# Orders drawn up anew, a narrow product of the state, and two transfers moved to ScalarE's queue, in an adaLN block with linear attention and an MLP

## The chip, the core and the metric

The kernel runs on one core of a Trainium2 chip. A core has five engines that run their own instruction streams: TensorE (PE, matmuls; its weight loads are listed apart as PEld), VectorE (DVE), ScalarE (ACT), GpSimd (POOL) and SyncE (SP), which here only issues transfers. ScalarE can issue transfers too, on a queue of its own. The metric is the device time of one execution in microseconds; the comparisons are of medians of several runs.

## What is computed

One block on S = 2048 tokens of D = 576 features, all in float32. The six modulation vectors come from one matrix product; then linear attention with 32 heads of 18 features, then an MLP with F = 4608.

```python
mod = (_silu(c) @ w_mod).reshape(c.shape[0], 6, 1, -1)
sa, ca, ga, sb, cb, gb = (mod[:, i] for i in range(6))
h = _layernorm(x) * (1 + ca) + sa
# attention: qkv of h @ wqkv; phi(t) = where(t > 0, t + 1, exp(t)) + 1e-6
kv  = einsum("bhsd,bhse->bhde", phi(k), v)     # the state, summed over the tokens
z   = einsum("bhsd->bhd", phi(k))
o   = einsum("bhqd,bhde->bhqe", phi(q), kv) / (einsum("bhqd,bhd->bhq", phi(q), z)[..., None] + 1e-6)
x = x + ga * (o @ wo)
h = _layernorm(x) * (1 + cb) + sb
x = x + gb * (_silu(h @ w1) @ w2)
```

## The kernel before

**Precision.** TensorE takes float32 operands in two ways here. Plain f32 products are two instructions each in the trace. All large products are done instead in fp32r, one instruction each, with every operand split into a rounded part "hi" and the rest "lo" = full - hi; a product is then hi x hi + hi x lo + lo x hi. ScalarE makes the hi part (a copy with rounding, `w_hi`, `split_h`, `k_split`, `split_w`), VectorE or GpSimd the lo part (a subtraction, `w_lo`, `sub_hi` at L121).

**Tiles.** The tokens are 16 tiles of 128, in four blocks of 512; the features are KC = 4 chunks of 128 and a fifth of 64.

**Head (0 to about 36 us).** ScalarE's queue issues two small transfers of c (L269, L270). SP's queue issues x's first two tiles (`load_x`, L260) and then w_mod: `load_mod_cols(k0, k1)` fetches columns of the four full chunks into `mods` (L287) and of w_mod's last 64 rows into `tmod` (L285, one transfer for each of the two pieces). It is called for the first HEAD = 2 column chunks, and again for the other three. Then come w_qkv (`load_w`) and the rest of x. TensorE runs warm-up matmuls on a tile of ones (`warm_up`, L412) while these land. VectorE adds up w_mod times silu(c) chunk by chunk (`mod_sum`, L360 for the first, L362 for the others), TensorE sums over the partitions (`mod_mm`, L371: `mod_tail` for tmod, then `mod_sums`), VectorE writes the columns (`mod_cols`, L381). With them the normalised and transposed x is modulated and split into hT, and the product for k of tiles 0 and 1 begins (`k_part`, L407). `A.activation(warm, ..., Exp)` (L431) makes ScalarE load the table of the exponential early.

**Attention, first pass (to about 216 us).** For each tile t: `k_proj`, `v_proj`, `q_proj` (their matmuls are in `x_passes`, L226) and the transposes of the next block (L214). `kv_mm(t)` (L588) adds this tile's part of the state: for each of five groups j of seven heads (126 columns) two matmuls, with v's hi and lo parts as weights. The moving operand of both is 256 columns wide: 128 of phi(k)'s hi part, then 128 of its lo part. The two halves of the result lie side by side in a bank of PSUM (`kvp`) and are added after the last tile (L720 and the line after it). So there are 16 x 5 x 2 = 160 matmuls.

**Attention, second pass (to about 345 us).** The state and w_o become one matrix per tile of features; GpSimd forms `prod` (L1195), `pn` (L752) and the copy of pn's last columns (L754) for each tile, TensorE transposes pn (L811) and multiplies (L226). Evacuations of the PSUM tiles `big` are L825 and, for the first MLP groups, L901.

**MLP (the rest).** Products by a scheme with sums of blocks of the operands (L1323 up, L1396 down, L1404 the additions into acc), with operands streamed back from DRAM.

**The order of the work.** TensorE runs in program order. For the other engines ORDERS holds an order by hand, up to about 402 us: number n is the engine's n-th instruction in the order in which the program states them, and `arrange` chains them in the order of the list. After that, `manual_schedule(engines=ENGINES)` runs all engines in program order. The numbers that are spoken of below:

- VectorE: 9 and 10 copies of silu(c)'s last part (L435), 14 ve (L183), 16 and 17 normalising x (L193), 18 mod_sum's first step (L360), 19 and 20 the next two; 21 and 31 mod_cols (L381); 24 to 27 mod_sum for the other columns; 29 and 30 w_lo of w_k's chunks 0 and 1 (L315), 43 of chunk 2; 33, 34, 36, 37 statistics of x (L178), 32 lo of hT's chunk 2 (L121); 76 to 79 normalising x of the next block, 123 a sum for the next modulation vectors (L519); 461 lo of the second-phase hT's chunk 3 (L121), 472 a sum of blocks (L1137), 477 and 465 other lo parts, 475, 484 and 483 additions into acc (L901).
- ScalarE: 3 the early exponential (L431), 11 the copy of tmod's last columns (L368), 15 and 17 hi of hT's chunks 2 and 3 (L205), 28 the exponential of the first k (L326), 30 and 31 hi of w_v's chunks 3 and 4.
- GpSimd: 28, 31, 35, 38, 42 prod, 29, 32, 36 pn, 30 and 33 pn's copies for tiles 2 and 3, 11 and 12 lo of w_v's chunks 3 and 4 (L315, L317).

Of the kernel before, what the change touches and what calls it, by code (L numbers as in the profile page):

```python
# [16 lines left out]
P = 128  # L17
# [5 lines left out]
def kernel(ctx: ExitStack, tc, A_x, A_wqkv, A_wo, B_x, B_w1, B_w2, c, w_mod, out):  # L23
# [7 lines left out]
    nc = tc.nc  # L31
# [4 lines left out]
    S, D = x.shape  # L36
# [6 lines left out]
    KC = D // P  # L43
    HG = 7 * DH
# [7 lines left out]
    def f32(ap):  # L52
# [1 line left out]

    ORDERS = {
        "PE": """
            0-105 114 106-108 115 109-113 116-2585
        """,
        "DVE": """
            2-3 1 0 4 6-7 11-12 8 5 13-14 18 15 9 16 10 17 19-24 29 25 28 26-27 30-31 43-44 33-34 36-37 35 38 32 39  # L60
            41 40 45 42 47 46 50 48-49 62-63 51 64 52 65-66 57 87 67 58 53 59 56 84-85 60 80 86 88 55 83 81 68-69 82
            70-72 122 73 54 74 61 89 75-76 123 78-79 91 77 90 92 124 93-94 96-97 125 98 126 100 127 99 95 103 101
            104-105 102 108 106-107 109-111 132-133 135 134 136 138-139 137 141-142 140 143-144 112-113 146-147 145
            114 148 117 115 149 118 116 119-121 128 131 129-130 150-151 224 222-223 225-226 152-154 157 155 158 156
            159 162 176 160-161 177-179 163 180 165 228 164 181 227 166-167 169-170 168 171-173 193-194 196 195 197
            199 198 200 202 201 203-205 174 206 175 207 182 185 209 183 208 186 188 187 210 184 189 192 190 211 191
            212-213 216 214 217 215 218 220 219 221 229-230 232-233 231 234-237 240 238-239 241-243 246 244 247 245
            248-249 252 250-251 253-255 258 256-257 259 262 260-261 263 266 268 267 270 269 271 264-265 272-273
            275-277 281 274 279 282 280 278 283-285 288 286 289 303 295-296 290 306 302 307 291 314 292 315 297 323
            298-299 293 308 300 324 294 304 331 309-310 287 311 301 312 305 332 316 340 313 317-321 341 325 322 351  # L70
            326-329 333 352 362 334-336 330 337 363 343-344 338 370 345-346 339 347 349 342 348 371 380 350 353-361
            381 398 364-369 372 399 416 373-375 377 376 378 417 424 385 382 384 379 387-388 391-392 394 425 402 386
            389 403 390 404-406 393 407 413 383 408 397 395 409-411 396 414 418 415 412 419-422 400-401 423 426-428
            432 429 431 430 435 433-434 437-440 445 441 446 442 444 443 436 447-451 454 452-453 455 469 466 456 467
            463-464 457 468 458 471 459-460 475 477 484 462 483 472 465 461 478 473 485 474 470 486 480 479 495 487
            482 488 492 481 490 476 493 489 491 494 500-501 497 503 529 499 496 498 510-511 502 506 504-505 507-509
            523 515 512-514 518 528 516-517 527 519 521-522 520 524-526 531 530 533 532 534-535
        """,
        "Activation": """
            0-2 4-9 11 10 3 12 16 19 13 15 14 18 21 17 20 26-27 24 22 29 23 28 25 30-33 55 35 37 59 39 58 42 40 38  # L80
            43 36 41 44 56-57 50 53-54 51-52 45 34 60-61 46 48 47 49 62-63 65-67 64 69 68 70 72 71 73-75 77-78 76 79
            81 80 82-84 93 85 95 87 86 96 88 94 89-92 97 99 98 100-102 104-105 103 106 108 107 109 149 110-112 152
            150-151 153 113-114 116-117 115 118 120 119 121-122 131 123-124 133-134 132 126 125 127-130 135 137 136
            138-139 141-142 140 145 143 146 144 147-148 154-155 157-158 156 159 161 160 162-182 184 183 186 185 188
            187 189-191 193-195 192 196-198 200 202 199 201 203-208 217 212 209 214 213 210 216 219 211 215 224 234
            220 218 239 221-222 225 223 245 235 231-232 256 226 228 230 233 227 229 236 240 237-238 270 241 243 246
            248-250 242 244 247 272 251-254 257 255 278 266 260 262-263 267 265 268 259 269 271 264 258 261 293 273
            305 274-276 281 283 282 277 284 279 307 285-287 296 289 280 288 290 292 291 301-302 299 297-298 303 300
            304 306 294-295 308-311 313 312 315-316 314 322-323 317 320 318-319 321 344 341 324 338 325-326 343 342
            327 339 345 328 330 329 340 332 331 347 333-334 336-337 335 348-349 346 353 350 354-356 351-352 358 357  # L90
            359 387 365 364 363 368 360-362 369 371 374 370 372 366 376 367 373 378 375 377 384 389 379 385 381 380
            382-383 386 388 390-395 397 396
        """,
        "Pool": """
            3 6 0 4-5 2 7 9 8 10-15 20 16-17 19 18 21-26 34 28 27 31 29-30 35 32 38 36 42 33 37 45 39-40 48 43-44 51
            46 41 47 55 49-50 58 52-53 61 85 56 73 57 54 59 77 60 62-63 80 64 74 65 68 75 69 78 66 72 70 79 67 76 81
            71 82-84 95 90-93 86-88 94 101 89 103 105 99-100 97 106-107 121 98 96 102 123 104 108-111 124 114 125
            113 112 115 118 116 119-120 117 122 126-128
        """,
        "SP": """  # L100
            0-25 57 30 26 31 29 32 27 39 28 55 33-34 56 53 40 54 41-46 35-38 47-52 61 63 58 64 60 66 62 59 65 67 69
            68 70-71 76 75 74 72-73 77-82 85 83-84 86-88 95 91 89 92 97 93 90 98 94 96 99-100 102 101 105 104 119
            103 118 117 106-107 110 108 112 109 111 113-116 123 120-122
        """,
    }

# [173 lines left out]
    def load_mod_cols(k0, k1):  # L280
        c0, c1 = k0 * P, min(k1 * P, D)
        for k in range(KC):
            if k == 2:
                for a in range(2):
                    nc.sync.dma_start(tmod[a * 64 : a * 64 + 64, 0, c0:c1], w_mod[KC * P : D, a * D + c0 : a * D + c1])  # L285
# [18 lines left out]
    def mod_ps(k):  # L304
        return kvp[k // 2][:, k % 2, :]
# [276 lines left out]
    def kv_mm(t):  # L582

        pkt, vt = pk[t % 2], vx[t % 2]
        for j in range(NHC):
            o = mod_ps(j)
            for h in range(2):
                T.matmul(  # L588
                    o, vt[:, j, h, :], pkt[:, :, j * HG : j * HG + P],
                    start=(t == 0 and h == 0 and j % 2 == 0), stop=(t == NT - 1 and h == 1),  # L590
                    skip_group_check=True,
                )
# [97 lines left out]
    with tc.manual_schedule(engines={mybir.EngineType.PE}):  # L690
# [77 lines left out]
        for j in range(KC + 1):  # L768
            psm = ps2()
            n = wo_rows[j]  # L770
# [780 lines left out]
        ws.update({g: Weights(g) for g in range(2, NG)})  # L1551
        for u in units[:2]:
            do_unit(*u)
    arrange()
    with tc.manual_schedule(engines=ENGINES):
        for u in units[2:]:
            do_unit(*u)
        for work, tokens in TAIL:
            unit.plain_down(work)
            run(tokens.split(), (unit, behind2), ())  # L1560
    psC.release()
    for p in (rs, ph, pf, pu, w2p, wqp, edge, wp, hTa, accp):
        p.release()
# [28 lines left out]
```

## Time and profile before

| | |
|---|---|
| median of 3 runs | 1142.06 us (1140.82 to 1143.03) |
| profiled execution | 1139.88 us, of it 1138.1 us from the first to the last instruction |
| TensorE clock granted | 1.000 |
| TensorE idle before its instructions, first 50 us / 200 to 402 us | 4.4 / 2.9 us |

The profile is of one execution. Section 1 of the page gives busy time per engine, section 4 the chain of work that ended last, followed back from the last instruction. In the timeline and in lists of groups a row has the start and length in microseconds, the engine, the line, the operation, what it writes and reads, and the count. A row of several instructions runs from the first start to the last end. A note in brackets tells how long the engine was idle before and who ended that. Matmuls are pipelined: the printed length of one is longer than the distance to the next.

### The profile page before, as it was taken

To read this page: it belongs to the slowest core of one execution; us is meant where nothing else is said; L and a number is where in the kernel's file an instruction comes from. 1 tells how busy PE (TensorE), PEld (TensorE's weight loads), DVE (VectorE), ACT (ScalarE), POOL (GpSimd) and SP (SyncE) were. 2 spreads that over 40 slices of the span, in tenths; PEclk is the share of its full clock that TensorE was granted. 3 is DMA by queue.
4 is the path that set the end of the run, shared out by engine and by line. 5 is a ranking of instruction groups with operands and counts; after the bars stand their busy time and mean duration, and the time that the engine had idled before them with its cause. 6 is when DMAs were issued, how large, how long until landed. Compare 5 with 4: busy or idle time off the path is not lost.

```text
span 1138.1 us, 19287 instructions
## 1 busy us (share of the span) xinstructions
PE 1126.6 (99%) x7033; PEld 1041.0 (91%) x7033; DVE 970.6 (85%) x1543; ACT 538.8 (47%) x1112; POOL 649.4 (57%) x743
## 2 busy tenths in 40 slices
PE   8999999999999999999999999999999999999998
PEld 8999999999998889999999999999999999999998
DVE  7866743685879889999999999999999999999996
ACT  6643442547556544445444444454454444444441
POOL 2100000373715767766775777677767767776776
PEclk9999999999999999999999999999999999999999
DMA  9521100223359976977968779769678697697684
GB/s 281 198 84 33 42 7 1 71 84 115 141 194 340 350 262 252 359 270 267 346 262 330 300 257 350 273 255 363 265 284 332 265 342 285 256 344 275 258 306 156
DMA packets 58813, 269.03 MB, mean 236 GB/s; under 512 B 5724, under 2 KB 21856, under 8 KB 35680
## 3 DMA queue, kind: packets, MB, share of 16 engines
q1 hardware_dynamic: 58708, 267.80, 63.8%
q8 instruction: 56, 0.92, 0.3%
q14 instruction: 37, 0.30, 0.1%
q10 hardware_dynamic: 12, 0.00, 0.0%
HBM read 250.12 MB, written 16.78 MB: 235 GB/s over the span
## 4 chain that ended last, share of the span: by engine, by line
PE 93%; DVE 2%; DMA 1%; POOL 1%; ACT 1%; issue 0%; DVEq 0%; POOLq 0%
PE up L1323 34%; PE down L1396 32%; PE psK L226 12%; PE big L226 6%; PE big L896 2%; PE small L885 2%; PE kvp L588 2%; PE small L214 1%; DMA hT<-hd 1%; PE big L811 1%; PE psT L214 1%; PE kvp L412 1%; DMA raw<-in_w_mod_dram 1%; PE up L1426 1%; PE down L1426 1%; POOL prod L1195 0%
## 5 line engine op out<-in xcount | busy, mean ns | idle before, releaser
L1404 DVE TENSOR_TENSOR acc<-down,acc 128x576 f32<-128x576 f32 x330 | 246.2, 753 | 14.6 <-PE down L1396 5.3
L1323 PE MATMUL up<-hT,w 128*128 128x512 f32 x916 | 239.4, 390 | 0.1
L1323 PEld LDWEIGHTS up<-hT,w 128*128 128x128 f32 x916 | 164.5, 188 | 25.0 <-DMA hT<-hd 0.3
L1358 POOL TENSOR_TENSOR s<-f,f 128x256 f32<-128x256 f32 x66 | 51.6, 782 | 162.0 <-ACT f L1339 162.0
L1396 PE MATMUL down<-w,hb 128*128 128x288 f32 x792 | 120.6, 294 | 0.0
L1396 PE MATMUL down<-w,hc 128*128 128x288 f32 x792 | 120.6, 294 | 0.0
L1396 PEld LDWEIGHTS down<-w,hb 128*128 128x128 f32 x792 | 113.8, 188 | 5.1
L1396 PEld LDWEIGHTS down<-w,hc 128*128 128x128 f32 x792 | 113.7, 188 | 5.1
L121 DVE TENSOR_TENSOR w<-v,w 128x288 fp32r<-128x288 f32 (+1 forms) x170 | 114.4, 682 | 0.5 <-ACT w L1057 0.5
L1404 DVE TENSOR_TENSOR U<-down,U 128x576 f32<-128x576 f32 x132 | 99.5, 754 | 17.5 <-PE down L1396 15.6
L226 PE MATMUL psK<-w,hT 128*128 128x352 f32 (+3 forms) x506 | 106.2, 336 | 0.5 <-POOL w L317 0.5
L1323 PE MATMUL up<-room,w 128*128 128x512 f32 x348 | 91.0, 390 | 0.0
L1377 POOL TENSOR_TENSOR hc<-s,hc 128x512 fp32r<-128x512 f32 x66 | 89.4, 1354 | 0.0
L226 PEld LDWEIGHTS psK<-w,hT 128*128 128x128 f32 x506 | 82.0, 189 | 6.8 <-POOL w L317 0.7
L1339 ACT ACTIVATE f<-f 128x512 f32<-128x512 f32 x102 | 64.4, 631 | 48.9 <-DVE f L1344 26.5
L184 POOL TENSOR_TENSOR rstd<-ve,neghalf 128x4 f32<-128x4 f32 (+3 forms) x10 | 9.8, 977 | 134.5 <-DVE ve L183 134.4
L1342 DVE TENSOR_TENSOR f<-up,p 128x512 f32<-128x512 f32 x102 | 69.6, 683 | 12.8 <-PE up L1323 11.9
L1065 ACT CAST w<-v 128x288 fp32r<-128x288 f32 x85 | 36.7, 434 | 75.4 <-PE down L1396 65.9
L1362 POOL TENSOR_TENSOR f<-f,s 128x256 f32<-128x256 f32 x66 | 50.7, 769 | 36.3 <-DVE hb L1377 25.9
L1323 PEld LDWEIGHTS up<-room,w 128*128 128x128 f32 x348 | 62.5, 188 | 9.4
L1396 PE MATMUL down<-w,hd 128*128 128x288 f32 x396 | 63.0, 294 | 0.9 <-DVE acc L1404 0.9
L1396 PE MATMUL down<-w,ha 128*128 128x288 f32 x396 | 63.0, 294 | 0.0
(310 smaller groups left out, 2529.4 us busy)
## 6 DMA issues: line engine op xcount, KB each, us to landing
hT<-hd SPq DMA_DIRECT2D x66, 1280.0 KB, 5.9
hT<-hd SPq DMA_DIRECT2D x45, 1024.0 KB, 5.3
room<-hd SPq DMA_DIRECT2D x35, 1280.0 KB, 5.6
room<-hd SPq DMA_DIRECT2D x20, 1024.0 KB, 5.3
v<-in_B_w_dram SPq DMA_DIRECT2D x17, 576.0 KB, 6.7
v<-in_B_w_dram SPq DMA_DIRECT2D x17, 512.0 KB, 7.0
hd<-S SPq DMA_DIRECT2D x6, 1024.0 KB, 4.3
xt<-in_A_x_dram SPq DMA_DIRECT2D x16, 288.0 KB, 3.1
```

Source lines behind the costliest of these rows:

```text
L121: return V.tensor_sub(lo, full, f32(hi))
L214: T.transpose(ps[:, i * P : (i + 1) * P], xt[i][:, cidx * P : (cidx + 1) * P], ident)
L226: T.matmul(ps, xpart(a), wpart(b), start=n == 0, stop=n == len(XW) - 1)
L1065: A.copy(self.w2[n][:, 0], src)
L1323: T.matmul(ps, left, right, start=first and m == 0, stop=m == len(seq) - 1, skip_group_check=True)
L1339: A.activation(self.f[i, k], self.f[i, k], AF.Silu)
L1342: V.tensor_add(f, self.bank[bank[1]], self.p1)
L1358: G.tensor_add(self.s[:, 0:1], half(i, 0, 1), half(i, 1, 1))
L1362: G.tensor_sub(half(i, 1, 0), half(i, 1, 0), self.s[:, 1:2])
L1377: eng.tensor_sub(t[:, :, 1, :], src, f32(t[:, :, 0, :]))
L1396: T.matmul(ps[:, p, :HALF], self.a[i, n][:, u, p * P : (p + 1) * P], self.w.w2[n][:, v], start=n in (1, 5, 7, 6) and j == 0, stop=j == 2, ...
L1404: V.tensor_add(dst, ps[:, :, :HALF], dst)
```

## The change

Three edits, and the lists of orders that go with them.

1. `kv_mm`: the matmul with v's lo part as weights (h = 1) takes only the 128 columns of phi(k)'s hi part; lo x lo is left out. The other stays 256 wide. The number of instructions is the same.
2. `load_mod_cols`: on its first call the two transfers of w_mod's last 64 rows are issued by ScalarE, behind c's two, in place of SP. ScalarE's numbers from 2 on grow by two, SP's from 6 on fall by two.
3. `arrange()` is called at the end, and TensorE's list has one number more.
4. The lists for VectorE, ScalarE, GpSimd and SP are new throughout; in TensorE's, two transposes stand one matmul later.

The first lines of each list and those that are spoken of, in the numbering of each version:

```diff
         "PE": """
-            0-105 114 106-108 115 109-113 116-2585
+            0-106 114 107-109 115 110-113 116-2586
         "DVE": """
-            2-3 1 0 4 6-7 11-12 8 5 13-14 18 15 9 16 10 17 19-24 29 25 28 26-27 30-31 43-44 33-34 36-37 35 38 32 39
-            41 40 45 42 47 46 50 48-49 62-63 51 64 52 65-66 57 87 67 58 53 59 56 84-85 60 80 86 88 55 83 81 68-69 82
-            70-72 122 73 54 74 61 89 75-76 123 78-79 91 77 90 92 124 93-94 96-97 125 98 126 100 127 99 95 103 101
...
-            432 429 431 430 435 433-434 437-440 445 441 446 442 444 443 436 447-451 454 452-453 455 469 466 456 467
-            463-464 457 468 458 471 459-460 475 477 484 462 483 472 465 461 478 473 485 474 470 486 480 479 495 487
+            0 3 2 1 4 6-7 11 8 12-13 9-10 14-16 18 17 5 19-22 30 23-24 28-29 25-27 43 31 44 33-34 36 35 37-38 32 39
+            41 40 42 45-47 50 48-49 62-63 51-53 57 84 64 55 58 65 59 86 66 85 87 60 56 80 67 88 81 83 68 82 69 71 70
+            72 122 73-74 61 89 54 75 78 76 90 77 79 123 91 124 92-93 96-97 125 98 94 126-127 100 99 95 101 103-104
...
+            440 445 441 446 443 442 444 447-451 455 454 453 452 466 456 467 469 457 464 471 458-460 475 472 462 461
+            463 478 473 477 484 483 485-486 479 468 480 474 487 470 465 493 488 495 490 476 489 482 492 481 491 494
         "Activation": """
-            0-2 4-9 11 10 3 12 16 19 13 15 14 18 21 17 20 26-27 24 22 29 23 28 25 30-33 55 35 37 59 39 58 42 40 38
+            0-4 6-8 11 9-10 12 5 13-14 18 21 15-16 20 19 17 23 28 22 29 24-25 31 26 30 27 32-33 37 34-35 38-39 57 59
...
         "Pool": """
-            3 6 0 4-5 2 7 9 8 10-15 20 16-17 19 18 21-26 34 28 27 31 29-30 35 32 38 36 42 33 37 45 39-40 48 43-44 51
+            6-7 0 3 8 2 4-5 9-15 20 16-17 19 18 21-27 34 28 31 29 35 30 32-33 38 36 42 37 39 45 48 40 43-44 51 46-47
...
         "SP": """
-            0-25 57 30 26 31 29 32 27 39 28 55 33-34 56 53 40 54 41-46 35-38 47-52 61 63 58 64 60 66 62 59 65 67 69
+            0-23 55 28-29 24 26 25 27 30 37 31-32 52 51 53-54 38-44 33-36 45-50 59 61 58 64 62 56 60 63 57 65 67 66
...
@@ load_mod_cols
                 for a in range(2):
-                    nc.sync.dma_start(tmod[a * 64 : a * 64 + 64, 0, c0:c1], w_mod[KC * P : D, a * D + c0 : a * D + c1])
+                    queue = nc.sync if k0 else nc.scalar
+                    queue.dma_start(tmod[a * 64 : a * 64 + 64, 0, c0:c1], w_mod[KC * P : D, a * D + c0 : a * D + c1])
@@ kv_mm
         for j in range(NHC):
-            o = mod_ps(j)
+            o = mod_ps(j).rearrange("p (a q) -> p a q", a=2)
             for h in range(2):
+                n = 2 - h
                 T.matmul(
-                    o, vt[:, j, h, :], pkt[:, :, j * HG : j * HG + P],
+                    o[:, :n], vt[:, j, h, :], pkt[:, :n, j * HG : j * HG + P],
@@ the end of the kernel
-    arrange()
     with tc.manual_schedule(engines=ENGINES):
...
             run(tokens.split(), (unit, behind2), ())
+    arrange()
     psC.release()
```

Numbers of ScalarE and SP in the text are those of the version before.

More of the change, by code (lines that the diff above doesn't have):

```diff
@@ L78 @@
+            529 500-501 499 497 496 498 510 503 502 511 507 506 504-505 508 515 509 514 527 513 512 518 528 519
+            516-517 523 520-522 524-526 531 530 533 532 534-535
         """,
         "Activation": """
[L80 to L82 removed]
```

56 lines of the change are left out of this document (28 added, 28 removed).

## The prediction

> **What bounds the kernel now.** I read the page first, then the list of TensorE's waits, then a table of stretches, and only then the timeline around each wait.
>
> ```profile
> span 1138.1 us, 19287 instructions
> ...
> PE 1126.6 (99%) x7033; PEld 1041.0 (91%) x7033; DVE 970.6 (85%) x1543; ACT 538.8 (47%) x1112; POOL 649.4 (57%) x743
> ...
> PE 93%; DVE 2%; DMA 1%; POOL 1%; ACT 1%; issue 0%; DVEq 0%; POOLq 0%
> ```
>
> TensorE is busy 1126.6 of 1138.1 us and has 93% of the chain that ended last. Time can leave this kernel in two ways only: TensorE does less, or it waits less. The waits are few:
>
> ```profile
> PE psK L407 <- DVE hT L121: 1.4, 1, 1.4
> PE big L811 <- POOL pn L754: 1.0, 1, 1.0
> PE down L1396 <- DVE acc L1404: 0.9, 1, 0.9
> PE small L885 <- DVE hT L121: 0.6, 1, 0.6
> PE psT L214 <- DVE xt L193: 0.3, 1, 0.3
> ```
>
> ```profile
> 50.00:100.00 50.00, 50.00 (x329) 47.37 (x329) 34.53 (x66) 19.90 (x39) 1.01 (x1) 1.00 0.20 62
> 345.00:369.00 24.00, 23.20 (x149) 21.11 (x148) 23.00 (x34) 14.63 (x28) 11.25 (x10) 1.00 0.91 332
> ```
>
> The columns are the length, then busy time of PE, PEld, DVE, ACT and POOL. From 50 to 100 us TensorE is never idle; a new order of the other engines has nothing to win there. At 345 to 369 us VectorE is busy 23.00 of 24.00 us, so there its order counts. The largest waits that an order can touch are in the head (L407, 1.4), at the first transposes of the second phase (L811, 1.0) and at L885 (0.6).
>
> **The narrow product.** kv_mm issues 160 matmuls (L588), 80 of which shrink from 256 to 128 columns. Both the product and its weight load are in the rows:
>
> ```profile
> L588 PEld LDWEIGHTS kvp<-pk,vx x160: 187/188/193, 36.4 to 203.2; 128*128 128x128 f32 x160
> L588 PE MATMUL kvp<-pk,vx x160: 277/282/496, 36.4 to 203.3; 128*128 128x256 f32 x160
> L371 PEld LDWEIGHTS kvp<-ones,hT x20: 186/192/192, 9.5 to 18.5; 128*128 128x128 f32 x20
> ```
> ```profile
> 36.36 1.26 PEld L588 LDWEIGHTS kvp<-pk,vx 128*128 128x128 f32 x10
> 9.50 0.97 PEld L371 LDWEIGHTS kvp<-ones,hT 128*128 128x128 f32 x8 [0.17 <-DVE hT L362]
> 9.50 1.10 PE L371 MATMUL kvp<-ones,hT 128*128 128x64 f32 x8
> 11.28 1.42 PEld L412 LDWEIGHTS kvp<-ones 128*128 128x128 f32 x12
> 386.81 1.82 PE up L1323 x8
> ```
>
> What a matmul costs in a stream is its pitch, not its printed 282 ns. Ten loads in 1.26 us, the last of them 0.19 long, give (1.26 - 0.19) / 9 = 119 ns for 256 columns; 512 columns take 1.82 / 8 = 228 ns. So 256 more columns cost 109 ns, and on that line 128 columns would come at 119 - 54 = 65 ns. But the plain f32 products of the head show a floor: 64 columns run at (0.97 - 0.19) / 7 = 111 ns (L371), and 128 columns at (1.42 - 0.19) / 11 = 112 ns (L412), the same for half the columns. Something that each pair of load and matmul has to go through takes 111 ns, and the load of kv_mm lasts as long (188) as theirs (192). I take 111 ns, since the weight tile is the same 128x128 of four bytes, and keep 65 ns as the other end: 80 x (111 - 119) = -0.6 us, against 80 x (65 - 119) = -4.3. The upper end is the pace of an f32 product, which is two such instructions, 2 x 112 = 224 ns: +8.4 us.
>
> A rule speaks for the floor: the Trainium skill, "TensorE: Matmul & The Clock Gate", section "LDWEIGHTS (loading the stationary operand)", lets a load take its columns over 1.2 GHz, 107 ns for 128. By it the sum of this part would be 80 x (107 - 119) = -1.0 us instead of -0.6, and the two f32 rows agree with it to 5 ns.
>
> **The two transfers on ScalarE's queue.** They leave SP's queue (1.18 us of issuing) and go behind c's two on ScalarE's, ahead of the table load and the silu:
>
> ```profile
> 1.40 0.70 ACTq L270 DMA_DIRECT2D crow<-in_c_dram  x1
> 2.13 1.28 ACT L430 ACT_TABLE_LOAD   x1 [2.13 <-issue]
> 3.00 1.18 SPq L285 DMA_DIRECT2D tmod<-in_w_mod_dram  x2
> 5.33 0.18 ACT L430 ACTIVATE sc<-psT 128x5 f32<-128x5 f32 x1 [1.92 <-PE psT L428]
> 7.97 0.53 PEld L371 LDWEIGHTS kvp<-z,tmod 128*128 128x128 f32 x4
> tmod<-in_w_mod_dram SPq DMA_DIRECT2D x2, 64.0 KB, 4.0
> ```
>
> At 0.70 each they push the table load to 3.5-4.8 us, and the silu waits for TensorE until 5.33 anyway: no cost while that 0.5 us of cover lasts, and up to 0.7 if each issue took twice as long. No gain either: tmod, issued at 3.0-4.2 and landing 4.0 later, is there by 7.6, while TensorE is in its warm-up matmuls until 7.97. What follows on SP's queue starts up to 1.2 us sooner, but VectorE, not a landing, sets the pace there, as the next rows show. I take 0.
>
> **The orders in the head.** VectorE's new list puts the copies of sc (9, 10) and ve (14) before mod_sum's first step (18), which stood ahead of GpSimd's power and filled its 1.00 us:
>
> ```profile
> 5.65 1.00 POOL L184 TENSOR_TENSOR rstd<-ve,neghalf 128x2 f32<-128x2 f32 x1 [1.63 <-DVE ve L183]
> 6.12 0.49 DVE L360 TENSOR_SCALAR hT<-hT,sc 128x512 f32<-128x512 f32 x1 [0.56 <-DMA hT<-in_w_mod_dram]
> 12.74 0.43 DVE L121 TENSOR_TENSOR hT<-raw,hT 128x256 fp32r<-128x256 f32 x1 [0.47 <-ACT hT L205]
> 17.09 0.75 DVE L315 TENSOR_TENSOR w<-acc,w 128x576 fp32r<-128x576 f32 x1
> 20.25 1.53 DVE L178 BATCH_NORM_STATS2 st<-xt 128x6 f32<-128x288 f32 x4
> 21.94 0.37 DVE L121 TENSOR_TENSOR hT<-raw,hT 128x256 fp32r<-128x256 f32 x1
> 29.55 1.82 POOL L317 TENSOR_TENSOR w<-acc,w 64x576 fp32r<-64x576 f32 x1
> ```
>
> Now 18 stands behind the power: ve some 0.25 later, and 0.49 of work that is no longer under it, less 0.3 for the two copies that no longer follow it: the first column sums are about 0.45 us late. Next, w_lo 1 (30, the 0.75 at 17.09) moves from a place where VectorE waited for TensorE to one ahead of five steps on the path; it takes over a wait of 0.47 there, so the second sums are 0.45 + 0.75 - 0.47 = 0.7 late. ScalarE then makes both casts (17, 15) after three modulations instead of the first of them (15) before. That is hidden: the four statistics at 20.25 still stand before chunk 2's difference at 21.94, so L407's wait of 1.4 us is not removed but takes some of the delay. What is late next is ScalarE's copy for GpSimd's two differences, and with them TensorE at L226: I take +0.8 us there. At 49.5 us the wait of 0.3 for xt goes, because 78, 76, 77 and 79 now precede 123, which waits for a transfer: -0.3. Head: +0.5 us, with -1 (the 1.4 us wait shrinks after all) and +2 (nothing of the delays is taken up) as its ends.
>
> **The orders later on.** GpSimd:
>
> ```profile
> 229.97 1.17 POOL L752 TENSOR_TENSOR pn<-acc,r 128x576 f32<-128x576 f32 x1
> 235.96 0.40 POOL L754 COPY pn<-pn 128x64 f32<-128x64 f32 x2
> ```
>
> The copy that ends pn of tile 3 (33) is ready at 231.14 but stands behind 38, 36 and 42 until 235.96, and TensorE waits for it. The new list has 33 ahead of these three. The wait goes: -1.0 us. Copy 30 now goes behind 35, one product of 1.4 us, and has about that much to spare.
>
> VectorE, at L885's wait:
>
> ```profile
> 352.81 0.62 ACT L1092 CAST hT<-S 128x512 fp32r<-128x512 f32 x1
> 353.61 0.76 DVE L901 TENSOR_TENSOR acc<-big,acc 128x576 f32<-128x576 f32 x1
> 355.92 1.76 DVE L1137 TENSOR_TENSOR S<-S 128x512 f32<-128x512 f32 x1
> 357.94 0.68 DVE L121 TENSOR_TENSOR hT<-S,hT 128x512 fp32r<-128x512 f32 x1
> 362.21 6.55 PE L896 MATMUL big<-w,hs 128*128 128x288 f32 x48
> ```
>
> Chunk 3's difference (461, at 357.94) could start at 353.4, when its cast ends. The new list moves it ahead of 477, 484, 483 and 465; it then ends near 356, before TensorE asks: -0.6 us. The price is that the two evacuations 484 and 483 (L901) go back by some 4 us, to about 360, with L896 needing their banks at 362.2. Between -0.7 and 0 (the wait moves on).
>
> All other moves trade places within work that TensorE does not wait for; the bound on them is the wait at L1396 that could go too (-0.9), and new waits, which no row can show (rival 4). The movement of the call of arrange and the one matmul more in TensorE's list change no order: 0.
>
> **Sum:** -0.6 + 0 + 0.5 - 1.0 - 0.6 = -1.7 us; the profiled execution's 1138.1 us of span becomes 1136.4. Around its span that execution has 1.8 us (1139.88), and the median of the three runs is 1142.06, 2.2 above it; I subtract from the median: **1140.4 us**, 0.15% less.
>
> **Rivals.**
>
> 1. The narrow product streams with no floor, at 65 ns: -4.3 instead of -0.6, -5.4 in all, 1136.7 us. For it speaks the straight line from 512 to 256 columns, against it the 64 columns at 111 ns, though those are f32, not fp32r. The Trainium skill, on the same page, section "Back-to-back issue gap", states 81 ns for pairs of load and matmul at 128 columns; by that figure this part would be -3.0 us.
>
> 2. The orders take more: L1396's 0.9 and 1.0 of L407's wait go too. -1.7 - 1.9 = -3.6, 1138.5 us. For it: both are waits for VectorE; against it: the statistics still stand ahead of chunk 2, and L1396 lies behind the end of the list.
>
> 3. Slower: below 256 columns an fp32r product falls back to the pace of an f32 one, 224 ns. Place: all 80 matmuls; +8.4 instead of -0.6, 1149.4 us. No fp32r product under 256 columns is in this trace, so no row excludes it; against it speaks that every fp32r row here is one instruction and every f32 one two. The other terms are -1.1, so it decides from (1.1 + 2.3) / 80 = 43 ns above 119, 162 ns, on.
>
> 4. Slower too: VectorE, full at 345 to 369 us, becomes the bound. Six evacuations (L901, 0.76) that now stand behind differences come too late for TensorE's banks: 6 x 0.76 = 4.6, instead of -0.6 there: 1145.6 us. Against it: 2 us of room before 362.2.
>
> 5. The orders do nothing: each wait that goes comes back at the next full engine, and only the product counts: 1141.5 us.
>
> **How the numbers follow.** 0.2%, 2.3 us, is about what a measurement of this kernel can tell from no change, so faster means under 1139.8. My forecast's own spread (head -1 to +2, the rest ±1) straddles that: of its 0.50, 0.20 is faster and 0.30 the same. Rival 1 has 0.15 and rival 2 0.10, both faster; rival 3 0.07 and rival 4 0.12, slower; rival 5 0.06, the same. Faster 0.45, same 0.36, slower 0.19. The range from 1135.5 to 1143.0 takes in rivals 1, 2 and 5 and leaves out 3 and 4.
>
> **What would show it.** The pitch of L588's narrow matmuls: 111, 65 or 224 ns. L811's wait on pn and L885's on hT gone. The first column sums about 0.45 us and the first L226 about 0.8 us later than 31.4. tmod landing earlier with no wait shortened by it. The forecast is wrong if a wait of over 1 us stands anywhere after 50 us, or if the head ends earlier than before.

## The result, and the profile after

The changed kernel takes 1138.5 us (median of 13 runs), the kernel before 1141.44 us in 13 runs beside it. The ratio is 0.9978 with a 95% interval from 0.9969 to 0.9988: 0.22% faster, or 2.5 us by the means of the two sets (the medians lie 2.9 us apart). The forecast was 1.7 us less, 1140.4 us; of the 1.9 us between that time and the measured one, 0.6 is the kernel before, which has 1141.44 us here and had 1142.06 in its three runs. The profiled execution took 1137.56 us, of it 1135.6 us of span; the one before 1138.1 us.

From the page of the changed kernel, the span, busy times and engine shares of the chain:

```profile
span 1135.6 us, 19288 instructions
...
PE 1125.4 (99%) x7033; PEld 1040.0 (92%) x7033; DVE 971.1 (86%) x1543; ACT 538.3 (47%) x1112; POOL 651.8 (57%) x743
...
PE 96%; DVE 1%; ACT 1%; DMA 1%; POOL 0%; issue 0%; DVEq 0%; POOLq 0%; ACTq 0%
```

TensorE works 1.2 us less, and the rest of the 2.5 us is waiting. Its waits, changed kernel:

```profile
PE psK L408 <- ACT hT L205: 1.3, 1, 1.3
...
PE kvp L372 <- ACT tmod L369: 0.7, 1, 0.7
PE psT L391 <- ACT xt L191: 0.6, 1, 0.6
PE psK L226 <- POOL w L318: 0.6, 1, 0.6
PE kvp L372 <- DMA tmod<-in_w_mod_dram: 0.5, 1, 0.5
...
PE psK L226 <- DVE acc L334: 0.4, 1, 0.4
PE big L898 <- DVE hs L121: 0.3, 1, 0.3
```

(Line numbers are one or two higher than before: L811 is now L813, L885 L887, L896 L898, L1396 L1398.) The waits at L811 (1.0), L1396 (0.9), L885 for hT (0.6) and at 49.5 us for xt (0.3) are gone. L407's 1.4 is L408's 1.3 and names ScalarE now. The last two rows are new. In the head, mod_tail's first wait for tmod (0.5) is new too, and its second, 0.4 for a transfer before, is 0.7 for ScalarE's copy, since ScalarE's new list has the table load (14.06 to 15.34 us) ahead of that copy. Both are covered, because the sums behind them need VectorE's results of 9.9 and 17.8 us.

Where time is won or lost is read best by one matmul at a time: TensorE issues 7033 matmuls in both kernels, so the start of its k-th one after, less the start of the k-th before, is a running account. From these two profiles:

| stretch, us | prediction | account moves by |
|---|---|---|
| 0 to 49 | +0.8 | +0.55 |
| 49.5, first transposes (L214) | -0.3 | -0.56 |
| 50 to 210, kv_mm, without 117 | -0.6 | -0.70 |
| 117, x_passes (L226) | 0 | +0.68 |
| 236, pn (L811) | -1.0 | -1.13 |
| 236 to 250 | 0 | +0.23 |
| 358, L885 | -0.6 | -0.85 |
| 364, L896 | 0 | +0.58 |
| 365 to 404 | 0 | +0.30 |
| 405, L1396 | 0 (rival 2: -0.9) | -1.13 |
| 1097, a transfer (L1323) | 0 | -0.39 |
| sum | -1.7 | -2.42 |

The 0.39 us at 1097 us is nothing of the change: in the profile of before a weight load there waits for a landing (`PEld up L1323 <- DMA hT<-hd: 0.3, 1, 0.3`). It waits in e1 and e9 below too, and in e3, e6 and e7, which change nothing there, it doesn't and the account falls by as much. Without this row the sum is -2.03. The two sums lie 0.7 us apart, 0.3 without it, the parts further.

### The profile page after: what moved, and what is told of

Its sections match the earlier page's. It is cut to its first block, busy times and chain, and to the rows that moved or that the text cites. A ratio compares the mean times of both kernels' runs of the same rounds, so it can differ in the third digit from the quotient of the medians.

```text
span 1135.6 us, 19288 instructions
## 1 busy us (share of the span) xinstructions
PE 1125.4 (99%) x7033; PEld 1040.0 (92%) x7033; DVE 971.1 (86%) x1543; ACT 538.3 (47%) x1112; POOL 651.8 (57%) x743
## 4 chain that ended last, share of the span: by engine, by line
PE 96%; DVE 1%; ACT 1%; DMA 1%; POOL 0%; issue 0%; DVEq 0%; POOLq 0%; ACTq 0%
PE up L1325 34%; PE down L1398 32%; PE psK L226 13%; PE big L226 7%; PE small L887 2%; PE big L898 2%; PE kvp L590 1%; PE big L813 1%; PE small L214 1%; PE up L1428 1%; PE down L1428 1%; PE psT L214 1%; DMA raw<-in_w_mod_dram 0%; DVE hT L363 0%; PE kvp L372 0%; PE psK L778 0%
## 5 line engine op out<-in xcount | busy, mean ns | idle before, releaser
L1398 PE MATMUL down<-w,hc 128*128 128x288 f32 x792 | 120.7, 294 | 0.0
L1398 PE MATMUL down<-w,hb 128*128 128x288 f32 x792 | 120.6, 294 | 0.0
L1398 PEld LDWEIGHTS down<-w,hc 128*128 128x128 f32 x792 | 113.7, 188 | 5.4 <-PE up L1325 0.3
L1398 PEld LDWEIGHTS down<-w,hb 128*128 128x128 f32 x792 | 113.7, 188 | 5.3
L226 PE MATMUL psK<-w,hT 128*128 128x352 f32 (+3 forms) x506 | 106.3, 336 | 1.0 <-POOL w L318 0.6
L226 PEld LDWEIGHTS psK<-w,hT 128*128 128x128 f32 x506 | 81.8, 188 | 7.4 <-POOL w L318 0.8
L1398 PE MATMUL down<-w,he 128*128 128x288 f32 x396 | 63.0, 294 | 0.0
L1398 PE MATMUL down<-w,ha 128*128 128x288 f32 x396 | 63.0, 294 | 0.0
```

The costliest lines, as they stand in the source:

```text
L226: T.matmul(ps, xpart(a), wpart(b), start=n == 0, stop=n == len(XW) - 1)
L1398: T.matmul(ps[:, p, :HALF], self.a[i, n][:, u, p * P : (p + 1) * P], self.w.w2[n][:, v], start=n in (1, 5, 7, 6) and j == 0, stop=j == 2, ...
```

## The experiments

Each kernel's profile was set against the one before in the same running account; "shift" means a step in it. Single times scatter by 2 us and more (the kernel before: 1139.66 to 1144.05), so the steps, not the times, decide. Where one time is given, the kernel ran once; e2, e3, e5 and e7 took 1136.58, 1140.04, 1139.2 and 1142.68 us, the kernel before 1141.28 beside the first two and 1141.54 beside the others.

**e1: the narrow product alone**, in the kernel before.

```diff
-            o = mod_ps(j)
+            o = mod_ps(j).rearrange("p (a q) -> p a q", a=2)
...
+                n = 2 - h
-                    o, vt[:, j, h, :], pkt[:, :, j * HG : j * HG + P],
+                    o[:, :n], vt[:, j, h, :], pkt[:, :n, j * HG : j * HG + P],
```

> The kernel before with the narrow product as its only edit. Theory of a floor (111 ns for each pair of weight load and matmul): a wide and a narrow matmul together take 231 ns in place of 239, so each kv_mm block is 0.04 us shorter and TensorE is 0.6 us earlier after the last of the 16 blocks. Rival, streaming without a floor: 119 + 65 = 184 ns for the two, 4.3 us earlier. Rival, pace of an f32 product: 119 + 224 ns, 8.4 us later. All waits of TensorE as in the kernel before, L1396's and L811's among them.

1140.2 us, before in that job 1141.28. From 54 to 202 us, with nothing else changed, the account falls from +0.62 to -0.13, 0.75 us in the 14 blocks of ten matmuls that lie there; over all 16 blocks it is 0.85. A narrow and a wide matmul together take 232 ns by their starts, where two wide ones took 240. The account of e1 stood at +0.6 us when it came to 54 us, although its head is that of the kernel before; more on that under e6.

**e2: where the floor is.** The changed kernel; from tile 4 on, every fourth tile has a narrower moving operand (64 columns) in its second matmul, every fourth a narrower weight tile (64 columns), every fourth only 128 moving columns in both. Parts of lo x hi, or hi x lo, are left out of the state there.

```diff
-                n = 2 - h
+                n, w, m = 2 - h, P, P
+                if t > 3 and h and t % 4 == 1:
+                    w = 64
+                if t > 3 and h and t % 4 == 2:
+                    m = 64
+                if t > 3 and t % 4 == 3:
+                    n = 1
...
-                    o[:, :n], vt[:, j, h, :], pkt[:, :n, j * HG : j * HG + P],
+                    o[:m, :n, :w], vt[:, j, h, :m], pkt[:, :n, j * HG : j * HG + w],
```

> The changed kernel, in which kv_mm takes other sizes for the token tiles from 4 on: tiles with t % 4 = 1 use 64 columns in the matmul with v's lo part (the other 64 are left out), tiles with t % 4 = 2 use 64 columns of weights there (half of its result is left out), tiles with t % 4 = 3 take 128 columns in both matmuls (hi x lo is left out), the others are as in the changed kernel. If the weight load is the floor: 231 ns for the two matmuls as they are, 231 with 64 moving columns, about 185 with 64 columns of weights, since that load takes some 53 ns less, and 222 with 128 columns in both. If the floor is one per instruction, whatever its size: 231 with 64 columns of weights too. If columns streamed decide: 184 as they are, 157 with 64 columns, 130 with 128 in both.

The weight loads of one tile each in e2's timeline: tile 5 (64 moving columns), tile 6 (64 weight columns), tile 7 (128 columns throughout):

```profile
107.03 1.23 PEld L596 LDWEIGHTS kvp<-pk,vx 128*128 128x128 f32 x10
```
```profile
120.55 1.17 PEld L596 LDWEIGHTS kvp<-pk,vx 128*128 128x128 f32 x10
```
```profile
133.94 1.20 PEld L596 LDWEIGHTS kvp<-pk,vx 128*128 128x128 f32 x10
```

and of one tile in the changed kernel:

```profile
53.88 1.23 PEld L590 LDWEIGHTS kvp<-pk,vx 128*128 128x128 f32 x10
```

The last of ten loads is 0.19 us long (0.13 with 64 columns), so the starts lie (1.23 - 0.19) / 9 = 116 ns apart in the first and the fourth, (1.17 - 0.13) / 9 = 116 in the second, (1.20 - 0.19) / 9 = 112 in the third. Halving the moving columns again wins nothing, and neither do half as many weight columns. At 128 and at 64 columns the pace is 109 to 113 ns for a load and its matmul, as the prediction took it. By the rule it quoted from the Trainium skill ("TensorE: Matmul & The Clock Gate", section "LDWEIGHTS (loading the stationary operand)") a load of 64 columns would take half of 107 ns; the load itself is indeed shorter (134 to 138 ns, where 128 columns take 190), but the pace isn't, so that rule is not what sets the floor.

**e3: TensorE's number 2586 and arrange at the end, alone**, in the kernel before.

```diff
-            0-105 114 106-108 115 109-113 116-2585
+            0-105 114 106-108 115 109-113 116-2586
...
-    arrange()
     with tc.manual_schedule(engines=ENGINES):
...
+    arrange()
     psC.release()
```

> The kernel before with arrange called at the end and TensorE's list one number longer, and nothing else. My prediction put this edit at nothing. Theory now: the number more ties TensorE's first matmul behind the lists, VectorE's first addition there then waits for its own matmuls and not for the next six, and TensorE's wait of 0.9 us at L1396 (404.7 us) goes: 1.1 us earlier from there to the end. Rival: VectorE's new order is what removed that wait, and here it stays.

TensorE's timeline in e3 where the list ends:

```profile
403.21 0.98 PE L1396 MATMUL down<-w,he 128*128 128x288 f32 x6
404.03 0.99 PE L1396 MATMUL down<-w,ha 128*128 128x288 f32 x6
404.85 1.53 PE L1323 MATMUL up<-hT,w 128*128 128x512 f32 x6
406.22 0.96 PE L1396 MATMUL down<-w,hd 128*128 128x288 f32 x6
```

and in the kernel before:

```profile
401.61 0.96 PE L1396 MATMUL down<-w,ha 128*128 128x288 f32 x6
402.40 1.53 PE L1323 MATMUL up<-hT,w 128*128 128x512 f32 x6
403.77 0.96 PE L1396 MATMUL down<-w,he 128*128 128x288 f32 x6
405.68 1.04 PE L1396 MATMUL down<-w,hd 128*128 128x288 f32 x6 [0.94 <-DVE acc L1404]
```

The two edits do change an order, TensorE's own. With its list ending at 2585, he came after ha and up, VectorE's addition of he could start only at 404.77, and hd waited for the bank. With 2586 he comes first, its addition runs under ha and up, and the shift at 405 us is -1.13 us. The instructions of all other engines stand in the same order in both.

**e5: which of the two does it.** The changed kernel with 2585 again, arrange left at the end.

```diff
-            0-106 114 107-109 115 110-113 116-2586
+            0-106 114 107-109 115 110-113 116-2585
```

> The changed kernel with one edit undone: TensorE's list ends at 2585 again, arrange stays at the end. Theory: the number 2586 alone ties the first matmuls of the later units (he at L1398) to the end of the list, and without it TensorE does six ha and six up products before them; VectorE's additions then come late and the wait of 0.9 us of TensorE for acc at 405 us is back, the end 1.1 us later than with 2586 (all up to 402 us as in the changed kernel, within the scatter of the first 50 us). Rival: it was VectorE's new list that took the wait away; then nothing changes at 405 us.

TensorE's timeline in e5:

```profile
402.18 1.53 PE L1325 MATMUL up<-hT,w 128*128 128x512 f32 x6
403.55 0.96 PE L1398 MATMUL down<-w,he 128*128 128x288 f32 x6
405.36 1.05 PE L1398 MATMUL down<-w,hd 128*128 128x288 f32 x6 [0.85 <-DVE acc L1406]
```

he is behind up again and the wait is back. The number does it, not the place of the call, and not VectorE's list. (e6 and e7 below also have the call at the end with the list at 2585, and TensorE's order in them is that of before.)

**e4, e6, e11: the two transfers and the head.** e4 is the changed kernel with the transfers on SyncE's queue, e6 the kernel before with only the transfers moved, e11 the changed lists with the wide product and SyncE's queue. The first edit of each:

```diff
-                    queue = nc.sync if k0 else nc.scalar
-                    queue.dma_start(tmod[a * 64 : a * 64 + 64, 0, c0:c1], w_mod[KC * P : D, a * D + c0 : a * D + c1])
+                    nc.sync.dma_start(tmod[a * 64 : a * 64 + 64, 0, c0:c1], w_mod[KC * P : D, a * D + c0 : a * D + c1])
```
(e6 has it the other way round; in e11 kv_mm is that of before as well.)

> The changed kernel with the two transfers of tmod back on SyncE's queue, the lists renumbered for it. If the move is worth nothing: the first column sums (L382 writes col_a) at 11.96 us again to 0.1 us, tmod landed by 7.5, the mod_tail matmuls at about 7.7 in place of 8.15 and then idle before the sums as long as VectorE needs, the end at the same time to 0.2 us. If the move pays: col_a later by up to 1.2 us, the time that the two take to be issued. If it costs: col_a earlier, by up to 0.5.

> The kernel before with only the two transfers moved to ScalarE's queue (numbers shifted, order otherwise as before). Read from the start of the first mod_sum step to be free of the scatter of the first landing: before, the third mod_sum step starts 6.3 us after it, the second column sums 10.9 to 11.2, L226's wait ends 23.5 to 23.8. Theory: the following transfers on SP's queue are issued 1.2 us sooner, and with them the later parts of the head come 0.3 to 0.4 us sooner (third step at 5.9 to 6.0). Rival, as predicted: nothing moves by more than 0.1, since VectorE sets the pace. In both, the two transfers themselves land later than 7.4 us though issued sooner.

> The changed kernel's lists with the wide product as before and the two transfers back on SyncE's queue. Theory: beside the changed kernel the pairs of matmuls of kv_mm come at 239 in place of 231 ns, so that the stretch from 54 to 202 us takes 0.6 us longer, and all else is the changed kernel's within the scatter of the first 50 us; in the head, read from the start of the first mod_sum step at L362, the second column sums come 11.1 to 11.5 us later and the first transposes at L214 41.5 to 42.3 later, against 41.9 to 42.6 with the order of before. Rival: e4's head (third step at +7.2, L214 at +42.3) comes again, which would be a cost of SyncE's queue under the new lists and so a gain of the move of 0.4 to 0.8 us.

1138.48, 1141.24 and 1140.35 us. The transfers in the changed kernel's timeline, and the products that wait for them:

```profile
2.13 1.18 ACTq L286 DMA_DIRECT2D tmod<-in_w_mod_dram  x2
3.34 1.28 ACT L431 ACT_TABLE_LOAD   x1 [3.34 <-issue]
...
8.15 0.68 PE L372 MATMUL kvp<-z,tmod 128*128 128x128 f32 x4 [0.50 <-DMA tmod<-in_w_mod_dram]
```

Issued 0.9 us sooner, the first of them lands sooner, at 6.26 us in place of 7.18, but the second doesn't: before it was there at 7.41 us, now mod_tail waits for it until 8.15 (until 8.93 in e10). Nothing comes of it either way, because mod_sums waits for VectorE until 9.9 us. In e6 it makes no difference at all: counted from the first step at L362, the third comes at +6.31 us as before, the second column sums at +10.9, the end of L226's wait at +23.5. In e4 the third step comes at +7.2, but e11, on the same queue with the same lists, has +6.75, and the changed kernel +6.76; e4's second step had waited 0.31 us for w_mod, a late landing. That e4 ends 1.0 us after the changed kernel has nothing to do with the head: at 410 us it stands 0.15 us ahead, and then it loses 1.2 us at 511 and 557 us, where TensorE waits for data that comes back from DRAM (`PE up L1324 <- DMA hT<-hd: 0.4, 1, 0.4`). e8, e10 and e11 lose 0.6 to 0.9 us in the same way.

For the head one profile of each kernel is not enough. These are the starts of TensorE's first matmul of L226 and of the first transposes at L214, in all profiles:

| lists in the head, queue | L226, us | L214, us | between |
|---|---|---|---|
| before, SyncE (before, e1, e3, e7) | 27.44, 28.06, 28.41, 29.28 | 49.83, 50.44, 51.01, 52.47 | 22.38 to 23.19 |
| before, ScalarE (e6) | 27.94 | 51.02 | 23.08 |
| after, ScalarE (after, e2, e5, e8, e9, e10, e12) | 27.99, 27.86, 29.38, 27.98, 28.36, 28.75, 28.09 | 49.88, 49.74, 51.18, 49.91, 50.25, 50.63, 49.97 | 21.80 to 21.93 |
| after, SyncE (e4, e11) | 28.72, 29.26 | 50.60, 51.19 | 21.88, 21.93 |

Up to L226 neither lists nor queue make a difference that stands out from a scatter of 1.5 to 2 us; the profile of before is its earliest case. It comes with the landings of the first transfers, but in e5 for the most part with TensorE: there the warm-up matmuls (L413) still come every 213 ns when the last of them starts at 9.88 us, where the other profiles have changed to 111 or 112 ns by 6.9 us, and the first column sums are 1.4 us later than the changed kernel's.

From L226 to L214 there is no scatter with the new lists and 0.5 to 1.3 us more with the old ones. Part of this comes back at the next product, because the new list has VectorE's evacuation behind the same sum that waits for a transfer. In e11:

```profile
50.15 1.42 DVE L519 SCALAR_TENSOR_TENSOR tmod<-raw,sc,tmod 128x1152 f32<-128x1152 f32 x1 [1.68 <-DMA raw<-in_w_mod_dram]
51.48 0.75 DVE L333 TENSOR_SCALAR acc<-psK 128x576 f32<-128x576 f32 x1
52.29 0.50 PE L226 MATMUL psK<-w,hT 128*128 128x512 f32 x1 [0.49 <-DVE acc L333]
```

The account rises there by 0.74 us in e11, by 0.40 in e8 and 0.29 in e10, and by less than 0.1 in the other six profiles with the new lists. Counted to this product, the stretch takes 22.16 to 23.02 us with the new lists and 22.80 to 23.60 with the old ones.

In e11 the stretch from 54 to 202 us runs flat at +2.06, so the 0.75 us there are the narrow product's and not the lists'.

**e7: GpSimd's list alone**, in the kernel before.

```diff
-            34 28 27 31 29-30 35 32 38 36 42 33 37 45 39-40 48
+            27 34 28 31 29 35 30 32-33 38 36 42 37 39 45 48 40
```

> The kernel before with GpSimd's new order of prod, pn and pn's copies alone (positions 26 to 42 of its list). Theory: TensorE's wait for pn at 235.9 us goes, -1.15 us from there on, and the gain stands until the end (the wait at L885 of 0.6 us may grow, by at most 0.3): 1.0 us off the end. Rival 5 of the prediction: what is won at 236 us comes back as longer waits at L885 and at L1396 by 405 us, nothing left.

The shift at 236 us is -1.14, as expected, and then +0.9 at 238. From e7's timeline:

```profile
236.27 0.75 DVE L748 TENSOR_REDUCE den<-prod 128x32 f32<-128x576 f32 x1 [0.65 <-POOL prod L1195]
236.94 0.45 DVE L178 BATCH_NORM_STATS2 st<-acc 128x6 f32<-128x288 f32 x1
237.81 0.76 DVE L121 TENSOR_TENSOR qT<-big,qT 128x640 fp32r<-128x640 f32 x1
238.72 2.90 PE L226 MATMUL big<-w,qT 128*128 128x288 f32 x20 [0.72 <-DVE qT L121]
```

VectorE's old list has den ahead of qT's lo part, and den now waits for a prod that GpSimd does later. In the changed kernel the lo part stands ahead:

```profile
234.46 0.76 DVE L121 TENSOR_TENSOR qT<-big,qT 128x640 fp32r<-128x640 f32 x1
234.63 0.71 PE L813 MATMUL big<-ident,pn 128*128 128x128 f32 x5
235.29 0.23 POOL L756 COPY pn<-pn 128x64 f32<-128x64 f32 x1
235.37 0.75 DVE L750 TENSOR_REDUCE den<-prod 128x32 f32<-128x576 f32 x1
235.37 2.88 PE L226 MATMUL big<-w,qT 128*128 128x288 f32 x20
```

So GpSimd's list is worth 0.2 us by itself and 0.9 (1.13 less 0.23) with the other new lists; that it is VectorE's which matters is read from these rows, since no run has VectorE's new list alone.

**e8: two places of VectorE's list mended**, in the changed kernel.

```diff
-            176 160 177-178 161 179-181 163 165 228 227 166-167 164
+            176 160-161 177-179 163 180 165 228 164 181 227 166-167
...
-            480 474 487 470 465
+            480 474 470 487 465
```

> The changed kernel with two places of VectorE's list mended: around 117 us the sums that wait for a transfer (L520) stand behind the evacuation 163 as before, and at 362 us the lo part 470 stands ahead of 487. Theory: the new wait at 117 us (0.4 idle, 0.3 to 0.7 of shift) and the one at L898 (0.3 idle, 0.3 to 0.6 of shift) go, and the end comes 0.7 to 1.2 us sooner than the changed kernel's; the median is 0.05 to 0.1% under it, 0.3% under the kernel before. Rival: the waits move to the next evacuation, VectorE being full there, and the time is that of the changed kernel.

1138.44 us (11 runs), ratio to before 0.9974 (0.9965 to 0.9983). The first mend works: in the changed kernel

```profile
115.22 1.41 DVE L520 SCALAR_TENSOR_TENSOR tmod<-raw,sc,tmod 64x1152 f32<-64x1152 f32 x1
116.80 0.75 DVE L334 TENSOR_SCALAR acc<-psK 128x576 f32<-128x576 f32 x1
117.61 0.50 PE L226 MATMUL psK<-w,hT 128*128 128x512 f32 x1 [0.41 <-DVE acc L334]
```

the evacuation at 116.80 stood behind a sum that waits for a transfer, and TensorE behind the evacuation; in e8, and in e9 and e10 with the same mend, there is no shift at 117 us. Without it the shift follows the landing of the transfer: 0.68 us in the changed kernel, 0.61 in e12, 0.43 in e5, 0.20 in e4, none in e2 and e11. The second mend doesn't work: the shift at 364 us is +0.57 as in the changed kernel. The time gained is within the intervals.

**e9: GpSimd's sum H ahead of its product on v**, with e8's first mend.

```diff
-            86-88 94 101 89 103
+            86-88 94 89 101 103
```

> The changed kernel with VectorE's list around 117 us mended as in e8 and, in GpSimd's list, the sum H (number 89, L1141) ahead of the product on v (101, L1008), which waits for a transfer until 358 us. Theory: at L898 VectorE's lo part hs is late because a VectorE operation on two SBUF operands and GpSimd's sum H shut each other out (1.33 to 1.54 us in place of 0.68 us), and H is late because 101 ahead of it waits 4 us for its transfer; with H first it runs near 354 to 356 us, the wait at L898 (0.3 idle, 0.57 us of shift) goes, and the end comes 0.5 us sooner than e8's. Rival: hs is late because VectorE's list as a whole is late there; then the shift of 0.57 us at 364 us stays, wherever H runs.

GpSimd, VectorE and TensorE around L898 in the changed kernel:

```profile
358.11 0.81 POOL L1008 TENSOR_TENSOR v<-v,bc_gb 128x288 f32<-128x288 f32 x1 [4.49 <-DMA v<-in_B_w_dram]
358.88 4.05 POOL L1141 TENSOR_TENSOR H<-H,S 128x512 f32<-128x512 f32 x1
...
361.94 1.54 DVE L121 TENSOR_TENSOR hs<-sl,hs 128x512 fp32r<-128x512 f32 x1 [0.17 <-ACT hs L890]
363.53 2.65 PE L898 MATMUL big<-w,hs 128*128 128x288 f32 x18 [0.32 <-DVE hs L121]
```

and in e9:

```profile
353.20 1.74 POOL L1141 TENSOR_TENSOR H<-H,S 128x512 f32<-128x512 f32 x1
...
362.30 0.68 DVE L121 TENSOR_TENSOR hs<-sl,hs 128x512 fp32r<-128x512 f32 x1
```

The same VectorE operation takes 1.54 us where it meets GpSimd's H and 0.68 where it doesn't. While VectorE has no pause, H doesn't get in; it takes 4.05 us and ends at 362.93, 1.2 us after VectorE's pause of 0.17 began, and hs, started at the end of the pause, ends 0.55 us after H. In e8 H met the earlier of the two hs (1.33 us, 358.79 to 360.12, beside H from 358.28 to 359.57), which is why the mend didn't help. The Trainium skill, "SBUF — State Buffer", section "SBUF: two separate sides", says of VectorE operations on two SBUF operands and of GpSimd's that whichever starts first has the shared ports for the whole instruction; these rows agree. With H first the wait of 0.3 us at L898 is down to 0.08, but the shift only from 0.57 to 0.35: theory and rival both hold a part, since VectorE is full from 359.56 until hs starts at 362.30. 1137.59 us (7 runs), ratio 0.9972 (0.9961 to 0.9982). That is the best figure here, but its interval covers the changed kernel's.

**e10: SyncE's list from position 101 on as before**, with e8's first mend. In the new list v's transfer (L1052) stands behind the load of xn, which can't start before 349.43 us; before it was issued at 339.34.

```diff
-            101-102 104 103 119 106-107 105 110 117 108 118 112 109 111
+            102 101 105 104 119 103 118 117 106-107 110 108 112 109 111
```
(The numbers are those of the version before.)

> The changed kernel with VectorE's list around 117 us mended as in e8 and SyncE's list from its position 101 on as before. Theory: it is SyncE's new order that made v's transfer (L1052) late, issued at 349.8 us in place of 339.3; with the old order GpSimd's product on v no longer waits, H runs before 357.5 us, and the wait at L898 goes as in e9 (0.5 us sooner than e8). Rival: the wait at L898 stays, or another transfer that the new order had brought forward is late instead and TensorE waits for it between 360 and 420 us.

1147.31 us (4 runs), ratio 1.0058 (1.0042 to 1.0074): the rival, and a hard one. From e10's timeline:

```profile
357.34 0.47 SPq L1045 DMA_DIRECT2D v<-in_B_w_dram  x1
...
371.69 1.66 ACT L1085 CAST S<-H 128x512 fp32r<-128x512 f32 x3 [7.13 <-DMA hd<-S]
372.34 0.69 DVE L121 TENSOR_TENSOR S<-H,S 128x512 fp32r<-128x512 f32 x1 [7.21 <-ACT S L1085]
...
373.75 1.57 PE L898 MATMUL big<-w,hs 128*128 128x288 f32 x5 [6.86 <-DVE acc L903]
```

SyncE's queue stands from 346.5 to 357.34 before the next load into a v buffer, which in SyncE's old order comes early and which VectorE's new order sets free late. Behind it the transfers that write S out start late (the first at 360.05 us, in the changed kernel at 357.09), ScalarE can't overwrite S, VectorE waits for ScalarE, and TensorE 6.86 us for VectorE's evacuation. Then TensorE's granted clock is 0.50 from 373.7 to 376.0 us, and the matmuls at L898 come every 240 ns in place of 131, which costs over 1 us more.

**e12: VectorE's numbers 451 to 461 as before**, in the changed kernel.

```diff
-            451 455 454 453 452 466 456 467 469 457 464 471 458-460 475 472 462 461
+            451 454 452-453 455 469 466 456 467 463-464 457 468 458 471 459-460 475 477 484 462 483 472 465 461
```

> The changed kernel with VectorE's list between the numbers 451 and 461 as before (461, the lo part of the second phase's chunk 3, stands again behind the evacuations 484 and 483 and behind 465), the rest of the list as changed. Theory: it is 461's new place that took the wait at L885 (L887 here) away; the wait for hT comes back, 0.6 to 0.9 us of shift at 358 us, and most of it stands until the end. Rival: the evacuations and lo parts that now come before 461 no longer stand in front of hs, so that the shift at L898 (0.57 us) shrinks as much and the sum of the two places is the same within 0.2 us.

1139.58 us, before in that job 1140.39, one run each. TensorE's waits in e12:

```profile
PE small L887 <- DVE hT L121: 0.9, 1, 0.9
PE big L898 <- DVE hs L121: 0.5, 1, 0.5
```

The lo part of chunk 3 in the changed kernel, and then in e12:

```profile
354.21 0.69 DVE L121 TENSOR_TENSOR hT<-S,hT 128x512 fp32r<-128x512 f32 x1
```
```profile
357.93 1.29 DVE L121 TENSOR_TENSOR hT<-S,hT 128x512 fp32r<-128x512 f32 x1
```

The wait for hT is back at its place: the account rises there by 0.3 us where the changed kernel's falls by 0.85. Half of the rival is true, for at 364 us, where the changed kernel loses 0.58, there is no shift. But L898's wait in the list above stands at 351 us, for an earlier hs, and between 349 and 355 us the account rises by 1.28. From 345 to 365 us it rises by 1.57 in all where the changed kernel's falls by 0.27, so the rival's sum is out.

## Why the prediction was right, and where it wasn't

The time lies in the range and on the forecast's side; the forecast was 0.8 us short of the gain, and two of its zeros were wrong in opposite directions.

- **Narrow product, -0.6.** Right in size (0.70 to 0.85) and in mechanism: the floor of 111 ns holds, and e2 shows that from 128 to 64 it depends on neither operand's columns. Rivals 1 and 3 fall.
- **Queue, 0.** Right, by the cover named. The sign "tmod landing earlier" came for the first of the two transfers alone; the second, which mod_tail waits for, landed no sooner.
- **Head, +0.5.** The predicted signs appeared: the first column sums 0.42 late, the second 0.64, L226's wait 0.61. They prove nothing: e1, with the old order, has +0.31, +0.62 and +0.62. The step that failed in this part was to take one profile's landings as the kernel's. The old list waits for w_mod at its first step (0.56 us in the row of before, 1.20 in e6), and the new one fills that time, which about pays for what it puts first. The -0.3 at 49.5 us is 0.5 to 1.3, since the old list made xt wait behind a sum that waits for a transfer, and that landing varies; but up to 0.74 of it comes back at the next product, where an evacuation now stands behind that sum. In the pair of profiles in the table the head comes to -0.01 in all (+0.55 and -0.56), where +0.5 was forecast.
- **L811, -1.0.** Right at its place (1.13); that it took VectorE's list as well (e7) was not in the prediction. Rival 5's idea, that such a wait comes back at the next full engine, is true of GpSimd's list alone.
- **L885, -0.6.** The wait went (0.85), and 0.58 came back at L898: the other end given, "the wait moves on". (With the old lists the wait for hT is 0.8 to 0.9 us in e1, e3, e6 and e7; the 0.6 was a small one.) It did not come back through the evacuations named there, but through hs. For 0.22 of it e9 shows the cause, GpSimd's late H behind a product whose transfer SyncE's new list starts 10 us later; the rest stays with H first, and that VectorE's full list is its cause is read from the rows. The prediction never followed SyncE's list. Rival 4 (4.6 us) did not come.
- **"The movement of the call of arrange and the one matmul more in TensorE's list change no order: 0."** This is the step that failed. The one number more brings he ahead of ha and up, 1.13 us, nearly half of the net gain. Rival 2 had the place and the size, but blamed VectorE, and the other half of it, L407, did not shrink; that its 1138.5 us is the measured median is chance.
- **New waits, 0.** 0.68 us at 117 us in the profile of the changed kernel: an evacuation put behind sums that wait for a transfer, the mistake that the new list mends for xt at 49.5 us. Its size is that of a landing, from none in e2 and e11 to 0.68.

Still open: the 0.23 us from 236 to 250 us and the 0.30 from 365 to 404, which the profile puts down to no wait of a matmul. For the first there is a candidate: a weight load of L226 stands idle for 0.25 us until 235.34, and qT's lo part, for which e7 waits at that place, ends at 235.22; that the two belong together isn't shown.

## What to carry to other kernels

Orders for several engines are one object: GpSimd's new order alone won 0.2 of 1.1 us, and SyncE's old order among new ones cost a wait of 6.9 us and some 9 us in all (1147.31 against 1138.44 in e8), so an order is judged with the queue behind every wait on a transfer or a buffer. A list's last number is an edit of order too: ask which instruction the first unlisted one may slip behind. An operation that waits for a transfer is best put behind whatever TensorE will ask for next. And before a difference in the first 50 us is explained, look for it in profiles that don't have the edit.

## What the hardware showed unasked

A VectorE operation on two SBUF operands and a GpSimd operation take turns, whole instructions at a time: 0.68 us became 1.33 to 1.54, and 1.29 became 4.05. A load with its matmul takes 109 to 113 ns whether either has 128 columns or 64. Of two transfers issued 0.9 us sooner through a second queue, the second landed no sooner, and in e10 1.5 us later. TensorE starts slowly: warm-up matmuls of one shape come every 213 ns at first and change to 111 or 112 ns between 4.0 and 6.9 us, in e5 not before the last at 9.88; and after 6.9 us without work, in e10, the granted clock was 0.50 for 2.3 us.
